# Turning a slot's rows with VectorE's 32x32 transposes in place of TensorE's, in a retention layer with a mixture of experts

## The chip, the cores and the metric

The kernel runs on one core of one Trainium2 chip. The metric is the device time of one execution in microseconds. Three runs of the kernel before took 399.4, 401.86 and 402.07 us, median 401.86.

## The reference, cut to what matters

Two layers follow each other. The first is retention over 4 batches, 8 heads, 768 positions and a head size of 64; the second sends each of the 3072 tokens (512 features) to one of 8 experts.

```
state = gamma * state + k[t] v[t]^T          # per batch and head
y[t]  = q[t] state / sqrt(64)
x     = y as 3072 rows of 512
logits = x @ w_gate + modality_bias[modality_id];  e = argmax(logits)
gate   = softmax(logits)[e]
out[rows of e] = gate * (relu(x[rows of e] @ w1[e]) @ w2[e])   # 512 -> 1024 -> 512
```

The order of the 512 features of `x` and of the rows of `w1` may be changed together without changing the product.

## The kernel before, in words

**Attention.** The 3072 tokens are 24 chunks of 128. For each chunk TensorE computes scores (`scores`, L168), products with the state (`heads_s`, L192) and with the masked scores (`heads_a`, L204), and VectorE masks the scores into `abuf` (L173) and writes the chunk's result `yT` (L211, features on partitions). `tokens_out` multiplies `yT` with an identity beside the gate's weights (L221), so that a chunk's rows and logits come out with tokens on partitions; ScalarE copies them into a tile `xs` in two halves (L225), VectorE reduces the logits (L226). ScalarE also scales the decay table into `dq` (L150), of which two buffers exist; chunk n's `dq` is read by `yT` of chunk n. From the third chunk on two chunks go together (`two_chunks`).

**Routing.** Per 6 chunks VectorE finds each token's expert and its place. GpSimd then writes the token's number and gate into the row and scatters the 128 rows of a chunk to `xsl` in HBM (L375). A row of `xsl` is 2176 bytes: four pieces of 128 features, each followed by 8 spare numbers; the first spare holds the token's number, the second its gate. `xsl` is divided into slots of 512 rows, each of one expert. The tile `xs` has ten buffers in rotation.

**Jobs.** A job is one slot through its expert. Two early jobs (`e0`, `e1`, full slots) and four from the final list (`f0` to `f3`) run in a row; a loop for further full slots exists. Two small remainders (`rest_...`, at most 32 rows) are computed inside the third and fourth job. A job has 32 stretches of six matmuls 128x128x512: 16 for `first` (L698, `w1`) and 16 for `second` (L716, `w2`). Each operand is split into a rounded part `hi` and a remainder `lo`, and three of their four products are taken. Beside them run, for the next job:
- `rows_in` (L646): SP loads the slot's 512 rows as four tiles `xg0` to `xg3` of 128 rows.
- `ids` (L656): VectorE copies the tokens' numbers and gates out of them, eight small copies.
- `raw` (L664) loads a weight block into one of four buffers; `cut` (L669) has ScalarE make `hi` (L672) and VectorE `lo` (L677).
- `flip` (L680), four calls: TensorE turns four 128x128 squares into one bank of PSUM (L683), ScalarE copies them to `hi` (L688), VectorE subtracts to get `lo` (L689).

At the end of a 128-row part of `second` ScalarE scales the result with the gate into `o` (L729), which uses the buffer of `xg0` to `xg3`, and GpSimd scatters it to the output (L730). `rest_flip` (L780) turns a remainder's 32 rows with four TensorE transposes (L781) and a ScalarE copy.

**Order.** On TensorE, ScalarE, VectorE and SP the order is that of the program text; GpSimd's instructions are pinned in order too. What belongs to a job is hung on named places: `at(n, where, ...)` puts a call at a place of chunk n, `on(q, ...)` at step q of a job (a step is two stretches, 16 steps to a job). The first job's `flip` calls stand at chunks 20 and 22, places "pr" (before `tokens_out` of the first chunk of the pair before) and "tk" (before that of the second); its `cut` calls at "end" of chunks 18 and 20, its `ids` at "end" of chunk 19. For every later job `rows_in` stands at step 5 of the job before it (step 1 for the second), `ids` at 8, `flip` at 8 and 9.

Of the kernel before, what the change touches and what calls it, by code (L numbers as in the profile page):

```python
# [7 lines left out]
F32 = mybir.dt.float32  # L8
F32R = mybir.dt.float32r
BF16 = mybir.dt.bfloat16  # L10
I32 = mybir.dt.int32
AF = mybir.ActivationFunctionType
ALU = mybir.AluOpType
AX = mybir.AxisListType

P = 128
B, H, S, D = 4, 8, 768, 64
NT, DM, NE, DF = B * S, H * D, 8, 1024
NCH = S // P
NN = B * NCH  # L20
NG = H // 2
GRP = 6
NGRP = NN // GRP
SLOT = 512
HH = SLOT // P
# [6 lines left out]
TAIL = 32  # L32
# [5 lines left out]
KC = DM // P  # L38
FC = DF // P
QW = KC * 256  # L40
LEAD = 12
XSB = 10
SINGLE = 2
XW = NG * (P + NE)
# [6 lines left out]
def kernel(  # L51
# [13 lines left out]
    nc = tc.nc  # L65
# [7 lines left out]
    wk = ctx.enter_context(tc.tile_pool(name="wk", bufs=2))  # L73
    me = ctx.enter_context(tc.tile_pool(name="me", bufs=1))
# [3 lines left out]
    def bank(name):  # L78
        return ps.tile([P, 512], F32, tag="bank", name=name)


    xsl = dr.tile([NONE + SLOT, XW], F32, name="xsl")
# [4 lines left out]
    ident = cst[:, C_ID : C_ID + P]  # L87
# [31 lines left out]
    def load_kq(n, split=False):  # L119
        tag = f"{('hi', 'lo')[n // 4 % 2]}{1 if n < 8 else 2}{n % 4}"  # L120
        t = me.tile([P, QW], F32R, tag=tag, name=f"kq_{n}")
        t = t.bitcast(F32).rearrange("p (i d) -> p i d", i=2)
# [512 lines left out]
    class Job:  # L635
        def __init__(self, tag):
            self.tag = tag
            self.raw, self.w, self.xT, self.hT = {}, {1: {}, 2: {}}, {}, []

    def reg(lst, i, hi):  # L640
        return nc.values_load(lst[0:1, i : i + 1], engines=[SP], min_val=0, max_val=hi)
# [2 lines left out]
        s.row, s.e = reg(lst, i, EMPTY) * SLOT, reg(lst, j, NE - 1)  # L644

    def rows_in(s):  # L646
        s.xg = [me.tile([P, XW], F32, tag=f"xg{hh}", name=f"xg{hh}_{s.tag}") for hh in range(HH)]
        src = xsl[bass.ds(s.row, SLOT), :].rearrange("(h p) w -> h p w", p=P)
        for hh in range(HH):
            ins = nc.sync.dma_start(s.xg[hh], src[hh])  # L650
            if s.tag[0] == "e":
                tc.add_to_no_dep_group("read_" + s.tag, ins.ins)
        if s.tag[0] == "e":
            reads.append("read_" + s.tag)

    def ids(s):  # L656
        s.tok = me.tile([P, HH], I32, tag="tok", name=f"tok_{s.tag}", bufs=2)
        s.gate = me.tile([P, HH], F32, tag="gate", name=f"gate_{s.tag}", bufs=2)
        for hh in range(HH):
            t = s.xg[hh]  # L660
            nc.vector.tensor_copy(s.tok[:, hh : hh + 1], t.bitcast(I32)[:, P : P + 1])
            nc.vector.tensor_copy(s.gate[:, hh : hh + 1], t[:, P + 1 : P + 2])

    def raw(s, m, i):  # L664
        src = w1 if m == 1 else w2
# [12 lines left out]
        s.w[m][i] = (hi, lo)  # L678

    def flip(s, kc):  # L680
        pb = bank(f"xp{kc}_{s.tag}")
        for hh in range(HH):
            nc.tensor.transpose(  # L683
                pb[:, hh * P : (hh + 1) * P], s.xg[hh][:, kc * (P + NE) : kc * (P + NE) + P], ident
            )
        t = me.tile([P, 2, SLOT], F32R, tag=f"xT{kc}", name=f"xT{kc}_{s.tag}")
        hi, lo = t[:, 0], t[:, 1]
        nc.scalar.copy(hi, pb)  # L688
        nc.vector.tensor_tensor(lo, pb, hi.bitcast(F32), op=ALU.subtract)  # L689
        s.xT[kc] = (hi, lo)  # L690

    def first(s, f, half):
        if half == 0:
# [17 lines left out]
    def second(s, hh, part):  # L711
        if part == 0:
            s.po = bank(f"o{hh}_{s.tag}")
        for f in range(2 * part, 2 * part + 2):
            for k, (a, wi) in enumerate(PAIRS):
                nc.tensor.matmul(  # L716
                    s.po, s.hT[f][a][:, hh * P : (hh + 1) * P],
                    s.w[2][f // 2][wi][:, (f % 2) * DM : (f % 2 + 1) * DM],
                    start=(f == 0 and k == 0), stop=(f == FC - 1 and k == 2),
                )  # L720
        if part == 3:
            o = me.tile([P, XW], F32, tag=f"xg{hh}", name=f"o{hh}_{s.tag}")[:, :DM]
            gate = s.gate[:, hh : hh + 1]
            if s is jobs[-1] and hh == HH - 1:
                h = DM // 2
                nc.vector.tensor_scalar(o[:, h:], s.po[:, h:], gate, None, op0=ALU.mult)
                nc.scalar.activation(o[:, :h], s.po[:, :h], AF.Copy, scale=gate)
            else:
                nc.scalar.activation(o, s.po, AF.Copy, scale=gate)  # L729
            ins = nc.gpsimd.indirect_dma_start(  # L730
                out=out[:, :],
                out_offset=bass.IndirectOffsetOnAxis(ap=s.tok[:, hh : hh + 1], axis=0),
                in_=o[:, :],
                in_offset=None,
                bounds_check=NT - 1,
                oob_is_err=False,
            )
            if s.tag != "dyn":
                disjoint(ins, "out_rows")
# [36 lines left out]
            nc.sync.dma_start(s.xg[g * TAIL : (g + 1) * TAIL], xsl[bass.ds(s.row, TAIL), :])  # L776

    def rest_flip(s):
        pb = bank("rxp")[:, : KC * TAIL].rearrange("p (c t) -> p c t", c=KC)
        for kc in range(KC):  # L780
            nc.tensor.transpose(  # L781
                pb[:, kc], s.xg[:TAIL, kc * (P + NE) : kc * (P + NE) + P], ident[:TAIL, :TAIL]
            )

        posf = me.tile([P, 1], F32, tag="rposf", name="rposf")
        nc.vector.tensor_copy(posf, s.xg.bitcast(I32)[:, P : P + 1])
        s.pos = me.tile([P, 1], I32, tag="rpos", name="rpos")
        nc.vector.scalar_tensor_tensor(s.pos, posf, 4.0, grp_t, op0=ALU.mult, op1=ALU.add)
        s.xT = wk.tile([P, KC, TAIL], F32, tag="s", name="rxT", bufs=3)
        nc.scalar.copy(s.xT, pb)  # L790

    def rest_first(s):
        ph = bank("rh")[:, :256]
# [50 lines left out]
    def at(n, where, fn, *args):  # L844
        hooks.setdefault((n, where), []).append((fn, args))
# [12 lines left out]
    for g in range(NGRP - 1):  # L858
        t = (g + 1) * GRP
# [8 lines left out]
        if early:  # L868
            at(t + 1, "end", early_b, g + 1)
            a, b = EARLY[g + 1]  # L870
# [5 lines left out]
    t = GRP * min(EARLY)  # L876
    at(t + 2, "st", taken_a)
    at(t + 2, "end", taken_b)
    e = jobs[0]
# [3 lines left out]
        at(t + 6 + 2 * i, "end", cut, e, 1, i)  # L883
        at(t + 7 + 2 * i, "top", raw, e, 2, i)
    at(t + 4, "sc", rows_in, e)
    at(t + 7, "end", ids, e)
    for kc in range(KC):
        at(t + 8 + kc // 2 * 2, ("pr", "tk")[kc % 2], flip, e, kc)

    def loads(n):  # L890

# [115 lines left out]
    def hooks_of(k):  # L1007

        hk = {}

        def on(q, fn, *args):
            hk.setdefault(q, []).append(lambda: fn(*args))

        s = jobs[k]
        for i in range(4):
            if k == 0 and i > 1:
                on(2 * i - 2, cut, s, 1, i)
                on(2 * i - 2, raw, s, 2, i)
            on(2 * i + 1, cut, s, 2, i)
        if k + 1 < len(jobs):  # L1020
            nxt = jobs[k + 1]
            on(1 if k == 0 else 5, rows_in, nxt)
            on(8, ids, nxt)
            for i in range(4):
                on(2 * i + 1, raw, nxt, 1, i)
                on(8 + i // 2, flip, nxt, i)
                on(9 + 2 * i, cut, nxt, 1, i)
                on(9 + 2 * i, raw, nxt, 2, i)
        if k == NEARLY - 2:

            on(3, gaps_room)
            on(6, gaps_a)
            on(7, gaps_b)
            on(7.5, gaps_c)
            for e in range(-1, NE):
                on(8 + (e + 1) / 2, gap, e)
        for s, load_in in zip(rests, (NEARLY - 1, NEARLY)):
            if k == load_in:
                on(7, rest_in, s)
                for i in range(8):  # L1040
                    on(7 + i, rest_load, s, 1 + i // 4, i % 4)
            if k == load_in + 1:
                on(0, rest_flip, s)
                on(2, rest_first, s)
                on(4, rest_mid, s)
                on(6, rest_second, s)
        if k == len(jobs) - 1:
            on(10, lambda: pin(nc.gpsimd.drain()))
        return hk
# [5 lines left out]
    with tc.manual_schedule(engines={PE, ACT, DVE, SP}):  # L1055
# [25 lines left out]
        r = last_tokens()  # L1081
# [7 lines left out]
    with tc.For_i(NLAST, nun, 1) as iv:  # L1089
        s = Job("dyn")  # L1090
        s.e = nc.values_load(
            lst[0:1, bass.ds(iv + U, 1)], engines=[SP], min_val=0, max_val=NE - 1
        )
        s.row = nc.values_load(
            lst[0:1, bass.ds(iv, 1)], engines=[SP], min_val=0, max_val=EMPTY
        ) * SLOT
        rows_in(s)
        ids(s)
        for kc in range(KC):
            flip(s, kc)  # L1100
        for m in (1, 2):
            for i in range(4):
                raw(s, m, i)
                cut(s, m, i)
        for i in range(32):
            stretch(s, i)


def _layout(inputs):
    import numpy as np  # L1110

    f = np.float32
# [10 lines left out]
    t = np.arange(S, dtype=np.float64) + 1.0  # L1123
# [7 lines left out]
    p = np.arange(P)  # L1131
    e = np.minimum(p // RUN, NE - 1)
# [8 lines left out]
    order = (head * D + np.arange(P) % D).reshape(DM)  # L1141
# [11 lines left out]
    mod = np.asarray(inputs["moe_modality_id"]).astype(np.int64).reshape(NN, P)  # L1153
    wg = inputs["moe_w_gate"][order].reshape(NG, P, NE).transpose(1, 0, 2)
    mb = np.broadcast_to(inputs["moe_modality_bias"].reshape(1, 2, NE), (P, 2, NE))
    w1 = inputs["moe_w1"][:, order].reshape(NE, KC, P, 4, 256).transpose(0, 3, 2, 1, 4)
    w2 = inputs["moe_w2"].reshape(NE, 4, 2, P, DM).transpose(0, 1, 3, 2, 4)
    arrs = {
        "qkv": np.stack([feat(k), feat(q), toks(k), toks(v)], axis=2),
# [45 lines left out]
```

## Time and profile before

| | |
|---|---|
| median of three runs | 401.86 us |
| profiled execution, its own time | 402.62 us |
| span of that execution | 400.8 us |
| mean granted TensorE clock | 0.994 of full |
| busy: TensorE / VectorE / ScalarE / GpSimd | 383.6 / 187.8 / 155.6 / 96.7 us |
| chain that ended last: TensorE / "issue" / DMA | 46% / 32% / 12% |

Busy time is summed over the span. A matmul's span overlaps the next one's, so TensorE's busy time says only when it had work. In a row of the timeline the columns are the start, the length, engine, line, operation, output from inputs, shape, count, and in brackets the idle time before it and what ended it. "issue" in the chain is time in which the engine waited for nothing that the profile shows.

### The profile page before, as it was taken

What the parts mean: (1) busy time and instruction counts of PE and PEld (TensorE: products, weight loads), DVE (VectorE), ACT (ScalarE), POOL (GpSimd) and SP (SyncE); (2) the same over time, 40 slices, a digit from 0 to 9 for tenths busy, and PEclk for the clock granted to TensorE, in tenths of its full rate; (3) what the DMA queues carried; (4) which work ended last, traced back from release to release, by engine and by line L of the source; (5) the groups of instructions that cost most, each with busy time, mean ns of one, the idle gap of its engine ahead of it and who ended that gap; (6) DMA issues with size and microseconds to landing.
All of it is one profiled execution on the core that took longest, in us unless ns stands there. A gap on an engine that the chain in (4) does not pass through costs nothing.

```text
span 400.8 us, 8169 instructions
## 1 busy us (share of the span) xinstructions
PE 383.6 (96%) x3067; PEld 323.2 (81%) x3067; DVE 187.8 (47%) x434; ACT 155.6 (39%) x305; POOL 96.7 (24%) x140
## 2 busy tenths in 40 slices
PE   4999999799999999999999999999999999999993
PEld 3999888698887888888877888878888888888882
DVE  1676858768649952445223352233622463234200
ACT  1255535336845432345223452334523443243110
POOL 1342581832810875000110001100011000100010
PEclk9999999899999999999999999999999999999999
DMA  7999899794545759367952579525343443400011
GB/s 273 398 385 398 303 339 400 239 390 174 198 147 189 248 184 330 116 216 243 370 201 81 198 243 359 214 71 199 105 159 105 156 166 131 151 35 0 15 39 50
DMA packets 27947, 82.32 MB, mean 205 GB/s; under 512 B 4861, under 2 KB 4989, under 8 KB 27649
## 3 DMA queue, kind: packets, MB, share of 16 engines
q1 hardware_dynamic: 22336, 66.09, 47.4%
q0 software_dynamic: 5136, 15.21, 9.8%
q8 instruction: 26, 0.43, 0.4%
q10 hardware_dynamic: 432, 0.46, 0.4%
q14 instruction: 17, 0.14, 0.1%
HBM read 65.42 MB, written 23.41 MB: 222 GB/s over the span
## 4 chain that ended last, share of the span: by engine, by line
PE 46%; issue 32%; DMA 12%; POOL 4%; DVE 3%; ACT 1%; POOLq 1%; SPq 0%; ACTq 0%
PE h_e L698 11%; PE o_e L716 11%; DMA kq<-in_qkv_dram 6%; DMA kv<-in_qkv_dram 6%; PE h_f L698 6%; PE o_f L716 5%; PE x L221 4%; POOL out_dram L730 3%; PE y L204 2%; PE sc L168 2%; PE y L192 1%; PE st L240 1%; PE xp_f L683 1%; PE xp_e L683 1%; DVE yT L211 1%
## 5 line engine op out<-in xcount | busy, mean ns | idle before, releaser
L698 PE MATMUL h_f<-xT_f,hi_f 128*128 128x512 f32 x256 | 81.3, 393 | 0.0
L716 PE MATMUL o_f<-hi_f,hT_f 128*128 128x512 f32 x256 | 79.4, 391 | 0.0
L677 DVE TENSOR_TENSOR lo_f<-raw_f,hi_f 128x1024 fp32r<-128x1024 f32 x32 | 39.2, 1224 | 49.5 <-ACT hi_f L672 45.3
L698 PEld LDWEIGHTS h_f<-xT_f,hi_f 128*128 128x128 f32 x256 | 48.1, 188 | 11.1 <-issue 1.2
L716 PEld LDWEIGHTS o_f<-hi_f,hT_f 128*128 128x128 f32 x256 | 47.6, 188 | 9.6
L706 DVE SCALAR_TENSOR_TENSOR hT_f<-h_f,hT_f 128x512 fp32r<-128x512 f32 x32 | 22.2, 692 | 66.4 <-ACT hT_f L705 66.4
L698 PE MATMUL h_f<-xT_f,lo_f 128*128 128x512 f32 x128 | 49.9, 390 | 0.0
L716 PE MATMUL o_f<-lo_f,hT_f 128*128 128x512 f32 x128 | 49.9, 390 | 0.0
L730 POOL DMA_INDIRECT out_dram<-o_f,tok_f x16 | 15.6, 972 | 132.6 <-ACT o_f L729 117.8
L698 PE MATMUL h_e<-xT_e,hi_e 128*128 128x512 f32 x128 | 40.5, 392 | 0.0
L705 ACT ACTIVATE hT_f<-h_f 128x512 fp32r<-128x512 f32 x32 | 19.2, 599 | 54.9 <-PE h_f L698 54.9
L716 PE MATMUL o_e<-hi_e,hT_e 128*128 128x512 f32 x128 | 39.8, 392 | 0.0
L173 DVE TENSOR_TENSOR abuf<-sc,cst 128x512 f32<-128x512 f32 x48 | 30.0, 681 | 17.4 <-PE sc L168 17.4
L156 POOL TENSOR_TENSOR vd<-kv,cst 128x512 f32<-128x512 f32 x24 | 24.9, 1045 | 42.5 <-PE y L204 13.5
L672 ACT CAST hi_f<-raw_f 128x1024 fp32r<-128x1024 f32 x32 | 33.4, 1045 | 0.0
L168 PE MATMUL sc<-kq 64*128 64x128 f32 x384 | 27.7, 293 | 5.4 <-DMA kq<-in_qkv_dram 5.2
L729 ACT ACTIVATE o_f<-o_f,gate_f 128x512 f32<-128x512 f32 x15 | 10.3, 689 | 55.0 <-PE o_f L716 43.6
L168 PEld LDWEIGHTS sc<-kq 64*128 64x128 f32 x384 | 24.6, 199 | 7.3 <-DMA kq<-in_qkv_dram 5.2
L221 PE MATMUL x<-wgt,yT 128*128 128x136 f32 x192 | 26.6, 287 | 3.1 <-DVE abuf L173 2.9
L225 ACT COPY xs<-x 128x272 f32<-128x272 f32 x48 | 18.4, 388 | 26.3 <-PE x L221 18.8
L716 PEld LDWEIGHTS o_f<-lo_f,hT_f 128*128 128x128 f32 x128 | 24.0, 188 | 5.0
L698 PEld LDWEIGHTS h_e<-xT_e,hi_e 128*128 128x128 f32 x128 | 24.0, 188 | 4.9
(172 smaller groups left out, 536.7 us busy)
## 6 DMA issues: line engine op xcount, KB each, us to landing
raw_f<-in_w_dram SPq DMA_DIRECT2D x32, 512.0 KB, 3.5
kq<-in_qkv_dram SPq DMA_DIRECT2D x23, 512.0 KB, 8.1
kv<-in_qkv_dram SPq DMA_DIRECT2D x19, 512.0 KB, 9.6
raw_e<-in_w_dram SPq DMA_DIRECT2D x16, 512.0 KB, 4.4
xg_f<-xsl SPq DMA_DIRECT2D x16, 272.0 KB, 4.4
abuf<-in_w_dram SPq DMA_DIRECT2D x8, 512.0 KB, 6.8
rw<-in_w_dram SPq DMA_DIRECT2D x16, 256.0 KB, 5.4
xg_e<-xsl SPq DMA_DIRECT2D x8, 272.0 KB, 4.2
```

Of the source, the lines that this page charges most:

```text
L156: nc.gpsimd.tensor_tensor(vds[n], vv, dec[:, n % NCH].unsqueeze(2).to_broadcast([P, H, D]), op=ALU.mult)
L168: nc.tensor.matmul(pe[j][:, g * P : (g + 1) * P], kt[r, g], qt[r, g], start=True, stop=True, skip_group_check=True,)
L173: nc.vector.tensor_tensor(a[:, j], pe[j].rearrange("p (h t) -> p h t", t=P), mask.unsqueeze(1).to_broadcast([P, NG, P]), op=ALU.mult,)
L221: nc.tensor.matmul(px[:, g], yT[:, 2 * u + g], wgt[:, 2 * u + g], start=(g == 0), stop=(g == 1), skip_group_check=True,)
L225: nc.scalar.copy(xs[:, 2 * u : 2 * u + 2], px)
L672: nc.scalar.copy(hi, t)
L677: nc.vector.tensor_tensor(lo, t, hi.bitcast(F32), op=ALU.subtract)
L698: nc.tensor.matmul(s.ph, s.w[1][f // 2][wi][:, o : o + P], s.xT[kc][a], start=(kc == 0 and k == 0), stop=(kc == KC - 1 and k == 2),)
L705: nc.scalar.activation(hi, s.ph, AF.Relu)
L706: nc.vector.scalar_tensor_tensor(lo, s.ph, 0.0, hi.bitcast(F32), op0=ALU.max, op1=ALU.subtract)
L716: nc.tensor.matmul(s.po, s.hT[f][a][:, hh * P : (hh + 1) * P], s.w[2][f // 2][wi][:, (f % 2) * DM : (f % 2 + 1) * DM], start=(f == 0 and k ...
L730: ins = nc.gpsimd.indirect_dma_start(out=out[:, :], out_offset=bass.IndirectOffsetOnAxis(ap=s.tok[:, hh : hh + 1], axis=0), in_=o[:, :], i ...
```

## The change

A job's rows are loaded as one tile `xb`, in which partition 32g + t holds, for each of 16 blocks of 32 rows, piece g (128 features) of row t of the block. VectorE turns the 32x32 squares of it, so that the features of one 128-row operand of the matmul are 32 from each of the four pieces; the rows of `w1` are laid out on the host in that order. The tokens' numbers and gates come by a load of their own (`tg`), and `ids` is gone. `flip` is divided: the transpose and ScalarE's copy stay at the old place, the subtraction `flip_lo` comes at a later one. The turned rows go through a buffer of the `xs` rotation. The output tile `o` is one for all four parts and shares its buffer with `xb`. `rest_flip` uses four VectorE transposes that write the operand directly.

```diff
+SQ = 32
+NB = SLOT // SQ
...
     def rows_in(s):
-        s.xg = [me.tile([P, XW], F32, tag=f"xg{hh}", name=f"xg{hh}_{s.tag}") for hh in range(HH)]
-        src = xsl[bass.ds(s.row, SLOT), :].rearrange("(h p) w -> h p w", p=P)
-        for hh in range(HH):
-            ins = nc.sync.dma_start(s.xg[hh], src[hh])
-            if s.tag[0] == "e":
+        s.xb = me.tile([P, NB, P], F32, tag="xb", name=f"xb_{s.tag}")
+        s.tg = me.tile([P, HH, 2], F32, tag="tg", name=f"tg_{s.tag}", bufs=2)
+        rows = xsl[bass.ds(s.row, SLOT), :]
+        src = rows.rearrange("(b t) (g e) -> g t b e", t=SQ, g=NG)
+        got = [
+            nc.sync.dma_start(s.xb[g * SQ : (g + 1) * SQ], src[g][:, :, :P]) for g in range(NG)
+        ]
+        got.append(
+            nc.sync.dma_start(s.tg, rows.rearrange("(h p) w -> p h w", p=P)[:, :, P : P + 2])
+        )
...
-    def ids(s):
-        s.tok = me.tile([P, HH], I32, tag="tok", name=f"tok_{s.tag}", bufs=2)
-        s.gate = me.tile([P, HH], F32, tag="gate", name=f"gate_{s.tag}", bufs=2)
-        for hh in range(HH):
-            t = s.xg[hh]
-            nc.vector.tensor_copy(s.tok[:, hh : hh + 1], t.bitcast(I32)[:, P : P + 1])
-            nc.vector.tensor_copy(s.gate[:, hh : hh + 1], t[:, P + 1 : P + 2])
...
     def flip(s, kc):
-        pb = bank(f"xp{kc}_{s.tag}")
-        for hh in range(HH):
-            nc.tensor.transpose(
-                pb[:, hh * P : (hh + 1) * P], s.xg[hh][:, kc * (P + NE) : kc * (P + NE) + P], ident
-            )
         t = me.tile([P, 2, SLOT], F32R, tag=f"xT{kc}", name=f"xT{kc}_{s.tag}")
-        hi, lo = t[:, 0], t[:, 1]
-        nc.scalar.copy(hi, pb)
-        nc.vector.tensor_tensor(lo, pb, hi.bitcast(F32), op=ALU.subtract)
-        s.xT[kc] = (hi, lo)
+        x = s.x[kc] = wk.tile([P, XW], F32, tag="xs", name=f"x{kc}_{s.tag}", bufs=XSB)[:, :SLOT]
+        nc.vector.transpose(
+            x.rearrange("p (b t) -> p b t", t=SQ), s.xb[:, :, kc * SQ : (kc + 1) * SQ]
+        )
+        nc.scalar.copy(t[:, 0], x)
+        s.xT[kc] = (t[:, 0], t[:, 1])
+
+    def flip_lo(s, kc):
+        hi, lo = s.xT[kc]
+        nc.vector.tensor_tensor(lo, s.x.pop(kc), hi.bitcast(F32), op=ALU.subtract)
...
-            o = me.tile([P, XW], F32, tag=f"xg{hh}", name=f"o{hh}_{s.tag}")[:, :DM]
-            gate = s.gate[:, hh : hh + 1]
+            if hh == 0:
+                s.o = me.tile([P, HH, DM], F32, tag="xb", name=f"o_{s.tag}")
+            o = s.o[:, hh]
+            gate = s.tg[:, hh, 1:2]
...
     def rest_flip(s):
-        pb = bank("rxp")[:, : KC * TAIL].rearrange("p (c t) -> p c t", c=KC)
-        for kc in range(KC):
-            nc.tensor.transpose(
-                pb[:, kc], s.xg[:TAIL, kc * (P + NE) : kc * (P + NE) + P], ident[:TAIL, :TAIL]
-            )
...
-        nc.scalar.copy(s.xT, pb)
+        for g in range(NG):
+            r, o = slice(g * TAIL, (g + 1) * TAIL), g * (P + NE)
+            nc.vector.transpose(
+                s.xT[r], s.xg[r, o : o + P].rearrange("p (c t) -> p c t", c=KC)
+            )
...
-    at(t + 7, "end", ids, e)
     for kc in range(KC):
         at(t + 8 + kc // 2 * 2, ("pr", "tk")[kc % 2], flip, e, kc)
+        at(t + 8 + kc // 2 * 2, ("tk", "end")[kc % 2], flip_lo, e, kc)
...
-            on(8, ids, nxt)
             for i in range(4):
                 on(2 * i + 1, raw, nxt, 1, i)
                 on(8 + i // 2, flip, nxt, i)
+                on(8.5 + i // 2, flip_lo, nxt, i)
...
-    w1 = inputs["moe_w1"][:, order].reshape(NE, KC, P, 4, 256).transpose(0, 3, 2, 1, 4)
+    w1 = inputs["moe_w1"][:, order].reshape(NE, NG, KC, SQ, 4, 256)
+    w1 = w1.transpose(0, 4, 1, 3, 2, 5)
```

## Rows read from the trace of the kernel before

**Rows 1.** The page, busy time of each engine (share of the span) and instructions.
```profile
PE 383.6 (96%) x3067; PEld 323.2 (81%) x3067; DVE 187.8 (47%) x434; ACT 155.6 (39%) x305; POOL 96.7 (24%) x140
```

**Rows 2.** Stretches: length, busy PE, PEld, DVE, ACT, POOL, clock, DMA share, GB/s.
```profile
96.00:112.00 16.00, 15.61 (x223) 13.85 (x222) 12.24 (x38) 10.54 (x30) 11.19 (x21) 1.00 0.48 172
112.00:394.00 282.00, 282.00 (x1452) 231.11 (x1450) 112.51 (x220) 101.80 (x150) 44.28 (x52) 1.00 0.48 166
```

**Rows 3.** The chain of waits in the jobs: start us, us, what.
```profile
181.03 0.87 PE xp_f L683 x8
...
204.63 0.36 PE rxp L781 x4
```

**Rows 4.** Timeline of VectorE, 98 to 106 us.
```profile
98.15 0.11 DVE L661 COPY tok_e<-xg_e 128x1 int32<-128x1 int32 x1
...
98.55 0.14 DVE L662 COPY gate_e<-xg_e 128x1 f32<-128x1 f32 x1
98.61 2.47 DVE L173 TENSOR_TENSOR abuf<-sc,cst 128x512 f32<-128x512 f32 x4
101.00 0.68 DVE L689 TENSOR_TENSOR xT_e<-xp_e,xT_e 128x512 fp32r<-128x512 f32 x1
...
102.31 0.20 DVE L226 TENSOR_REDUCE lg<-xs 128x8 f32<-128x32 f32 x1
103.83 1.23 DVE L677 TENSOR_TENSOR lo_e<-raw_e,hi_e 128x1024 fp32r<-128x1024 f32 x1 [1.33 <-ACT hi_e L672]
104.97 1.41 DVE L211 TENSOR_TENSOR yT<-y,dq 128x256 f32<-128x256 f32 x4
```

**Rows 5.** Timeline of ScalarE, 98 to 104 us.
```profile
98.64 0.59 ACT L688 CAST xT_e<-xp_e 128x512 fp32r<-128x512 f32 x1 [2.03 <-PE xp_e L683]
99.15 0.81 ACT L225 COPY xs<-x 128x272 f32<-128x272 f32 x2
...
101.59 1.27 ACT L150 ACTIVATE dq<-dcq,cst 128x128 f32<-128x128 f32 x4
102.77 1.03 ACT L672 CAST hi_e<-raw_e 128x1024 fp32r<-128x1024 f32 x1
```

**Rows 6.** Timeline of TensorE, 105 to 112 us.
```profile
105.53 1.17 PE L221 MATMUL x<-wgt,yT 128*128 128x136 f32 x8 [0.19 <-DVE yT L211]
...
110.93 1.19 PE L221 MATMUL x<-wgt,yT 128*128 128x136 f32 x8
111.87 0.48 PE L698 MATMUL h_e<-xT_e,hi_e 128*128 128x512 f32 x1
```

**Rows 7.** Timelines of GpSimd, SP, VectorE, TensorE in the jobs; the output's landing.
```profile
160.27 0.98 POOL L730 DMA_INDIRECT out_dram<-o_e,tok_e  x1 [2.67 <-ACT o_e L729]
...
170.94 0.33 SPq L650 DMA_DIRECT2D xg_f<-xsl  x1
...
185.77 1.29 DVE L689 TENSOR_TENSOR xT_f<-xp_f,xT_f 128x512 fp32r<-128x512 f32 x2 [0.51 <-ACT xT_f L688]
...
204.92 0.50 PE L698 MATMUL h_f<-xT_f,hi_f 128*128 128x512 f32 x1
...
out_dram<-o_e,tok_e POOLq DMA_INDIRECT x8, 5.5
```

**Rows 8.** TensorE's wait before 73.41, and the stretch around it as in rows 2.
```profile
73.41 0.73 PE L221 MATMUL x<-wgt,yT 128*128 128x136 f32 x4 [2.88 <-DVE abuf L173]
...
72.00:80.00 8.00, 6.59 (x98) 5.88 (x100) 5.28 (x18) 3.11 (x10) 6.70 (x14) 0.79 0.73 208
```

**Rows 9.** VectorE's groups by line and form: count, busy us, mean ns.
```profile
L256 DVE COPY wgt<-cst 128x512 f32<-128x512 f32 x1 | 0.4, 420 | 0.0
```

**Rows 10.** First job's row loads on SP, their landing, the stretch as in rows 2.
```profile
86.80 1.95 SPq L650 DMA_DIRECT2D xg_e<-xsl  x4
...
DMA to landing us min/median/max: 2.7/4.2/7.3
...
84.00:92.00 8.00, 8.00 (x148) 7.34 (x142) 4.62 (x12) 3.56 (x12) 2.09 (x2) 1.00 1.02 401
```

More of the change, by code (lines that the diff above doesn't have):

```diff
@@ L637, in __init__ @@
             self.tag = tag
-            self.raw, self.w, self.xT, self.hT = {}, {1: {}, 2: {}}, {}, []
+            self.raw, self.w, self.x, self.xT, self.hT = {}, {1: {}, 2: {}}, {}, {}, []
     def reg(lst, i, hi):
@@ L646, in rows_in @@
     def rows_in(s):
-        s.xg = [me.tile([P, XW], F32, tag=f"xg{hh}", name=f"xg{hh}_{s.tag}") for hh in range(HH)]
-        src = xsl[bass.ds(s.row, SLOT), :].rearrange("(h p) w -> h p w", p=P)
-        for hh in range(HH):
-            ins = nc.sync.dma_start(s.xg[hh], src[hh])
-            if s.tag[0] == "e":
+        s.xb = me.tile([P, NB, P], F32, tag="xb", name=f"xb_{s.tag}")
[8 more added lines that the diff above has]
+        )
+        if s.tag[0] == "e":
+            for ins in got:
                 tc.add_to_no_dep_group("read_" + s.tag, ins.ins)
-        if s.tag[0] == "e":
             reads.append("read_" + s.tag)
-    def ids(s):
-        s.tok = me.tile([P, HH], I32, tag="tok", name=f"tok_{s.tag}", bufs=2)
-        s.gate = me.tile([P, HH], F32, tag="gate", name=f"gate_{s.tag}", bufs=2)
-        for hh in range(HH):
-            t = s.xg[hh]
-            nc.vector.tensor_copy(s.tok[:, hh : hh + 1], t.bitcast(I32)[:, P : P + 1])
-            nc.vector.tensor_copy(s.gate[:, hh : hh + 1], t[:, P + 1 : P + 2])
     def raw(s, m, i):
@@ L731, in second @@
                 out=out[:, :],
-                out_offset=bass.IndirectOffsetOnAxis(ap=s.tok[:, hh : hh + 1], axis=0),
-                in_=o[:, :],
+                out_offset=bass.IndirectOffsetOnAxis(ap=s.tg.bitcast(I32)[:, hh, 0:1], axis=0),
+                in_=o,
                 in_offset=None,
@@ L1097 @@
         rows_in(s)
-        ids(s)
         for kc in range(KC):
             flip(s, kc)
+            flip_lo(s, kc)
         for m in (1, 2):
```

## The prediction

> **What bounds the kernel now.** I read the page's totals first: TensorE is busy for 96% of the span, VectorE for 47% [rows 1]. That is a mean over two stages, so the table by stretches comes next. From 112 us to 394 us, the expert jobs, TensorE is busy for all 282 us at full clock and VectorE for 112.5 us of them; in the 16 us before, where attention ends and the first job's rows are turned, TensorE is still busy for 15.6 us but VectorE for 12.2 and ScalarE for 10.5 [rows 2]. The chain of waits tells how close each stretch is. In the jobs it runs through TensorE alone, the transposes included [rows 3]. Around 100 us it is different: the three engine timelines show TensorE, ScalarE and VectorE handing work to each other within fractions of a microsecond, all three in written order [rows 4 to 6]. So an instruction taken off TensorE is worth its full time in the jobs, and perhaps nothing, or less, around 100 us.
>
> **What leaves TensorE in the jobs.** Eight transposes (two calls of `flip`) hold TensorE for 0.87 us in the chain, twice per job [rows 3]. Five jobs (the second early one and the four from the final list) are turned inside this stretch: 10 x 0.87 = 8.70 us. `rest_flip` holds it for 0.36 us [rows 3], twice: 0.72. Together **-9.42 us**.
>
> **What is added there, and its cover.** Per job VectorE gets four transposes and loses the eight small copies of `ids`; `flip_lo` is the old subtraction from another source, ScalarE's copy likewise. What they produce is finished at 187 and first used at 204.92 [rows 7], so some 18 us of other matmuls hide them. Without that cover each would cost its own duration. The same cover takes a late row load: SP issues the rows at 170.9 and they are wanted from 181.0 [rows 3, 7]; if they come late VectorE and ScalarE stand still, behind them wait `cut` and the output scaling, and behind `cut` SP's weight loads, but TensorE wants none of it before 204.92. The output tile now shares the row tile's buffer, so SP's row loads wait for the last output scatter of the job before: issued at 160.27, done 0.98 later, landed 5.5 after that, 166.8 [rows 7], still before 170.9. `rest_flip`'s four VectorE transposes replace a ScalarE copy two steps (5 us) ahead of their use. SP issues five loads for four and the pieces are shorter. The turned rows take buffers of the `xs` rotation, which GpSimd's scatters free: by order the third takes chunk 12's, scattered at chunk 20, one pair earlier. All this I cost at 0.
>
> **What happens around 100 us.** This is the step that I expect to give most of the gain back. Before, the first job's `flip` was TensorE, then ScalarE's copy, and the copy ran at 98.64 beside VectorE's mask products (98.61 to 101.0) [rows 4, 5]. Afterwards the copy needs VectorE's transpose, which stands behind those products in VectorE's order. I follow that order as the changed code writes it, with the durations of the old rows and one transpose at 0.68 us.
> First pair of chunks. Without `ids` (98.15 to 98.61) VectorE is free at 101.0 - 0.46 = 100.54. Then, each waiting for the one before: transpose 0.68, ScalarE copy 0.59, two `xs` copies 0.81, the logits' reduction 0.20, `flip_lo` 0.68, transpose 0.68, copy 0.59, two `xs` copies 0.81, four `dq` 1.27, `cut`'s copy 1.03, `cut`'s subtraction 1.23, the second `flip_lo` 0.68: 9.25 us [rows 4, 5]. Neighbours on one engine overlap a little (four products of 0.68 take 2.47 [rows 4]), so I take 9.0: `yT`, at 104.97 before, starts at about **109.6**.
> Second pair. Four `yT` 1.41, then transpose, copy, `xs` copies, reduction, `flip_lo` (0.68 + 0.59 + 0.81 + 0.20 + 0.68) twice, less the second reduction, which lies beside, then half of `yT` 0.42 before TensorE may start `x`: 7.55, with the overlaps 7.5: **117.1** where TensorE began it at 110.93 [rows 6]. That is a delay of **+6.2 us** for all that follows. TensorE's own work between, 105.53 to 110.93 less the transposes, is 4.5 us [rows 6] and fits underneath. The first job's 16 transposes (16 x 0.87 / 8 = 1.74 us) leave TensorE here too, and I count nothing for them: it would only wait longer.
> The clock. TensorE will stand still from about 103.4 to 110. [...]
>
> **The unknown prices.** No row shows a VectorE 32x32 transpose. From below: a plain copy of 128x512 takes 0.42 [rows 9]. From above: 16 blocks, each paid like the smallest VectorE instruction at 0.14 [rows 4], 2.24. I take the 0.68 of a 128x512 pass with one result per element, which it is nearest to in columns and type. Four stand in the chain, so the ends are -1.0 and +6.2 us.
> [...]
> The row load of the first job turns 512 rows of 2176 bytes into 2048 pieces of 512 bytes and 512 of 8. It was issued at 86.8 and landed at most 7.3 us after an issue, with the engines at 401 GB/s [rows 10]. If speed goes by bytes it lands near 95, hidden by 5 us, cost 0. If each piece takes as long as a whole row did, 1.1 MB at 401 GB/s is 2.8 us and three more such are 8.4: about 104, 3.5 us after VectorE wants it.
>
> **The sum.** The profiled execution took 402.62 us. 402.62 - 9.42 + 6.2 + 0.8 = 400.2. It stands 0.76 above the median of the runs, so against 401.86 I predict **399.4 us**, 0.6% faster.
>
> **The rivals.**
> 1. The whole gain. If VectorE and ScalarE find slack around 100 us that I don't see, the delay is nothing, and the first job's transposes leave TensorE's path too, 1.74 us. 402.62 - 9.42 - 1.74 = 391.5, or 390.7 against the median. For it: TensorE busy 96%. Against it: VectorE's order, in which the reduction that waits for ScalarE stands between the two transposes. Chance 0.15.
> 2. Slower: a costly transpose. [...] It decides from the point where four excesses over 0.68 eat the 2.4 us: 1.28 us per transpose. For it: no row of the kind. Against it: the plain 128x512 forms are all below 0.7. Chance 0.10.
> 3. Late rows. The small pieces land at 104 and VectorE stops the whole chain by 3.5 us: 403.7, or 402.9. For it: the engines were full when the load was issued. Against it: 13.7 us from issue to use. Chance 0.13.
> That the transposes would not leave TensorE can't be: the instructions are gone from the code.
>
> **Chances and range.** My forecast has 0.62; its own range is 396 to 402.5 (a transpose of 0.42 with no clock loss gives 397.6, hand-offs a little shorter 396; one near 1.2, 401.5). What can be told from no change is 1% of the median, 4 us: 397.8 to 405.9. Faster: rival 1 and a quarter of the forecast, 0.15 + 0.16, rounded to 0.32. Slower: most of rival 2 and what the others leave, 0.11. Within 1%: 0.57. The range 394 to 404.5 takes in the forecast, rival 3 and the cheaper half of rival 2; rival 1 lies outside.
>
> **What would show it.** Right: TensorE without transposes and gapless from the first `h` matmul to the end, over about 272.6 us instead of 282; the first `h` matmul near 118 to 119 instead of 111.87; `yT` of the 21st chunk near 109.6 with VectorE waiting for ScalarE's `xs` copies between two transposes; a granted clock under 1 between 104 and 120. Wrong: a first `h` matmul at 112 or before (rival 1); transposes over 1.3 us (rival 2); VectorE waiting for the row tile's DMA at 100 us (rival 3); or TensorE waiting inside the jobs, which would mean that the cover of 18 us isn't there.

## The result and the profile after

The changed kernel took **397.43 us** (median of 6 runs, 397.03 to 397.94), the kernel before on the same chip 401.16 us (6 runs, 399.4 to 402.07): ratio 0.9897, 95% interval 0.9882 to 0.9912. The prediction was 399.4 us and no change beyond 1%; the change gained 1.0%. The profiled execution took 397.86 us, 4.76 less than that of before.

The page of the changed kernel, the totals that answer to [rows 1]: busy time, share of the span, instructions.
```profile
PE 373.9 (94%) x2963; PEld 314.7 (79%) x2963; DVE 202.8 (51%) x418; ACT 156.5 (40%) x303; POOL 97.8 (25%) x140
```
TensorE has 104 instructions fewer: 96 transposes of the six jobs and 8 of the two remainders.

The table by stretches of the changed kernel, columns as in [rows 2]; the last row is the stretch of the jobs.
```profile
96.00:112.00 16.00, 10.53 (x126) 9.44 (x126) 10.19 (x25) 7.17 (x19) 9.53 (x19) 0.87 0.51 173
...
104.00:108.00 4.00, 0.51 (x10) 0.27 (x6) 1.66 (x3) 2.78 (x8) 3.31 (x8) 0.97 0.46 173
108.00:112.00 4.00, 3.15 (x14) 3.18 (x15) 2.74 (x8) 2.41 (x7) 1.09 (x1) 0.50 0.69 237
112.00:116.00 4.00, 4.00 (x60) 3.42 (x61) 2.43 (x6) 2.36 (x7) 0.84 (x1) 0.67 0.48 104
...
118.00:390.00 272.00, 271.63 (x1361) 222.05 (x1360) 125.64 (x209) 102.43 (x147) 45.10 (x52) 1.00 0.55 168
```
In the jobs TensorE is as full as before: the trace has no wait of it from 118 to 390 us. From 96 to 112 us its busy time fell from 15.61 to 10.53 us, though it lost only 16 transposes there (1.74 us): it stands still from 104.51 to 108.85 (the wait of 4.34 us below), and then runs at a granted clock of 0.50 from 108 to 112 and 0.67 from 112 to 116.

VectorE's timeline of the changed kernel, answering to [rows 4], and in its last row to VectorE's of [rows 7] (start, length, engine, line, operation, shape, count, idle time before it and what ended it).
```profile
97.43 2.44 DVE L175 TENSOR_TENSOR abuf<-sc,cst 128x512 f32<-128x512 f32 x4
99.79 0.70 DVE L685 STREAM_TRANSPOSE x_e<-xb_e 128x512 f32<-128x512 f32 x1
101.75 0.21 DVE L228 TENSOR_REDUCE lg<-xs 128x8 f32<-128x32 f32 x1 [1.26 <-ACT xs L227]
...
102.48 0.71 DVE L685 STREAM_TRANSPOSE x_e<-xb_e 128x512 f32<-128x512 f32 x1
104.44 0.20 DVE L228 TENSOR_REDUCE lg<-xs 128x8 f32<-128x32 f32 x1 [1.26 <-ACT xs L227]
106.54 1.23 DVE L678 TENSOR_TENSOR lo_e<-raw_e,hi_e 128x1024 fp32r<-128x1024 f32 x1 [1.90 <-ACT hi_e L673]
107.69 0.68 DVE L693 TENSOR_TENSOR xT_e<-x_e,xT_e 128x512 fp32r<-128x512 f32 x1
108.29 1.41 DVE L213 TENSOR_TENSOR yT<-y,dq 128x256 f32<-128x256 f32 x4
...
115.37 1.80 DVE L213 TENSOR_TENSOR yT<-y,dq 128x256 f32<-128x256 f32 x4 [0.30 <-PE y L206]
...
191.83 1.29 DVE L693 TENSOR_TENSOR xT_f<-x_f,xT_f 128x512 fp32r<-128x512 f32 x2
```
ScalarE's timeline of the changed kernel, answering to [rows 5].
```profile
100.53 0.62 ACT L688 CAST xT_e<-x_e 128x512 fp32r<-128x512 f32 x1 [4.64 <-DVE x_e L685]
101.05 0.67 ACT L227 COPY xs<-x 128x272 f32<-128x272 f32 x2
```
The two engines take turns as the prediction wrote it out. VectorE transposes at 99.79; ScalarE, which did the same copy at 98.64 before, now waits 4.64 us for that; VectorE then waits 1.26 us for ScalarE's `xs` copies before it comes to its next transpose. The first `yT` of the second pair of chunks starts at 108.29 instead of 104.97.

TensorE's timeline of the changed kernel, answering with its first row to [rows 8], then to [rows 6], and with the last two to TensorE's row of [rows 7] and to the end.
```profile
72.69 0.73 PE L223 MATMUL x<-wgt,yT 128*128 128x136 f32 x4 [2.88 <-DVE abuf L175]
...
97.23 2.12 PE L223 MATMUL x<-wgt,yT 128*128 128x136 f32 x16
...
108.85 3.96 PE L223 MATMUL x<-wgt,yT 128*128 128x136 f32 x16 [4.34 <-DVE yT L213]
...
116.56 1.19 PE L223 MATMUL x<-wgt,yT 128*128 128x136 f32 x8
117.50 0.48 PE L701 MATMUL h_e<-xT_e,hi_e 128*128 128x512 f32 x1
...
206.51 0.39 PE L701 MATMUL h_f<-xT_f,hi_f 128*128 128x512 f32 x1
...
389.24 0.39 PE L719 MATMUL o_f<-lo_f,hT_f 128*128 128x512 f32 x1
```
One group of 16 matmuls that took 2.12 us at 97.23 takes 3.96 at 108.85, behind the wait of 4.34 us. The first `h` matmul is at 117.50 instead of 111.87.

**Where the 4.76 us came from.** Split both executions at VectorE's becoming free of the mask products (100.54 before, without `ids`; 99.79 after), at the first `h` matmul, and at the start of the last `o` matmul (393.80 before, 389.24 after). Up to the first split: -0.75 us. From there to the first `h`: 11.33 before, 17.71 after, **+6.38**. Jobs: 281.93 before, 271.74 after, **-10.19**. Behind them: 8.82 before, 8.62 after, -0.20. Sum -4.76. The first term isn't the change's: TensorE's wait of 2.88 us ended at 73.41 before [rows 8] and ends at 72.69 after, 0.72 earlier, and the first instruction of the change, the row load, is issued at 85.71. The trace has the difference as early as 13 us: two groups of matmuls (`y` and `st` of the first chunks) took 1.97 and 1.01 us before, 1.68 and 0.63 after, and the `sc` matmuls behind them start at 13.76 and 13.04. E1 and E2 below, which hold most of the change, start those at 13.63 and 13.79, so this differs from execution to execution. In the experiments below VectorE comes free between 99.1 and 101.2 us.

### The profile page after: what moved, and what is told of

Its sections match the earlier page's. It is cut to its first block, busy times and chain, and to the rows that moved or that the text cites. A ratio compares the mean times of both kernels' runs of the same rounds, so it can differ in the third digit from the quotient of the medians.

```text
span 396.1 us, 7938 instructions
## 1 busy us (share of the span) xinstructions
PE 373.9 (94%) x2963; PEld 314.7 (79%) x2963; DVE 202.8 (51%) x418; ACT 156.5 (40%) x303; POOL 97.8 (25%) x140
## 4 chain that ended last, share of the span: by engine, by line
issue 56%; PE 24%; POOL 8%; DVE 6%; DMA 3%; ACT 1%; POOLq 1%; ACTq 0%; DVEq 0%
PE x L223 6%; POOL out_dram L735 5%; PE sc L170 5%; PE y L206 4%; PE h_e L701 4%; PE y L194 2%; PE st L242 2%; DMA kv<-in_qkv_dram 2%; DMA cst<-in_consts_dram 1%; POOL xsl L623 1%; POOL vd L158 1%; DVE x_e L685 1%; DVE abuf L175 1%; DVE lo_e L678 1%; ACT xs L227 1%
## 5 line engine op out<-in xcount | busy, mean ns | idle before, releaser
L735 POOL DMA_INDIRECT out_dram<-o_f,tg_f x16 | 15.5, 972 | 127.2 <-ACT o_f L734 116.9
L223 PE MATMUL x<-wgt,yT 128*128 128x136 f32 x192 | 28.0, 300 | 7.2 <-DVE yT L213 4.3
L223 PEld LDWEIGHTS x<-wgt,yT 128*128 128x128 f32 x192 | 25.1, 202 | 9.2 <-issue 4.7
```

The costliest lines, as they stand in the source:

```text
L223: nc.tensor.matmul(px[:, g], yT[:, 2 * u + g], wgt[:, 2 * u + g], start=(g == 0), stop=(g == 1), skip_group_check=True,)
L735: ins = nc.gpsimd.indirect_dma_start(out=out[:, :], out_offset=bass.IndirectOffsetOnAxis(ap=s.tg.bitcast(I32)[:, hh, 0:1], axis=0), in_=o, ...
```

## The experiments

Two sets of four kernels each ran beside the kernel before: 401.86 us in the first set (E1 to E4, 7 runs), 402.43 in the second (E5 to E8, 11 runs). Compare ratios, therefore, where sets differ. "Hand-offs" is the time from the first transpose of the first job (for the kernel before, VectorE's becoming free) to the first `h` matmul, "jobs" from there to the start of the last `o` matmul, both from the profiled execution.

| kernel | median us | ratio, 95% interval | hand-offs | jobs |
|---|---|---|---|---|
| before | - | 1 | 11.33 | 281.93 |
| changed | 397.43 | 0.9897 (0.9882 to 0.9912) | 17.71 | 271.74 |
| E1 first job on TensorE | 390.73 | 0.9719 (0.9703 to 0.9735) | - | 271.71 |
| E2 other order | 390.34 | 0.9705 (0.9687 to 0.9722) | 9.44 | 271.77 |
| E3 only the first job on VectorE | 406.99 | 1.0101 (1.006 to 1.0142) | 17.87 | 280.57 |
| E4 TensorE kept busy | 397.2 | 0.9888 (0.9871 to 0.9904) | 16.67 | 271.76 |
| E5 later transposes twice | 398.51 | 0.9897 (0.9878 to 0.9915) | 17.40 | 271.73 |
| E6 first transposes twice | 400.27 | 0.9944 (0.9928 to 0.996) | 19.66 | 271.76 |
| E7 remainders on TensorE | 399.82 | 0.9929 (0.9912 to 0.9946) | 17.65 | 272.99 |
| E8 other buffer | 398.44 | 0.9903 (0.9885 to 0.992) | 17.56 | 271.77 |

**E1 and E3: which job gains, which loses.** E1 turns the first job's rows on TensorE again, E3 those of all other full jobs instead (`on_pe` there is `s is not jobs[0] and s.tag != "dyn"`). A job turned by TensorE is loaded with tokens on partitions, still in pieces of 512 bytes, and its `w1` comes from a second copy in the old order of rows.
```diff
+    def on_pe(s):
+        return s is jobs[0]
...
     def flip(s, kc):
+        if on_pe(s):
+            pb = bank(f"xp{kc}_{s.tag}")
+            for hh in range(HH):
+                nc.tensor.transpose(pb[:, hh * P : (hh + 1) * P], s.xg[:, hh, kc], ident)
+            nc.scalar.copy(t[:, 0], pb)
+            nc.vector.tensor_tensor(t[:, 1], pb, t[:, 0].bitcast(F32), op=ALU.subtract)
...
-        src = w1 if m == 1 else w2
+        src = w2 if m == 2 else w1p if on_pe(s) else w1
```


> The changed kernel, but the first job alone is turned by TensorE again: its rows come with tokens on partitions in 512-byte pieces, its w1 from a second copy in the old order. Theory (the loss is the first job's turning on VectorE, in its written order around 100 us): the first h matmul comes near 111, the 10.2 us that the jobs gained stay, about 391 us. Rival A (the loss comes from the other parts of the change, the shorter pieces, the extra load of tokens and gates, the shared output buffer): the first h matmul stays near 117.5 and the time near 397.

> The reverse of the first: the first job is turned by VectorE as in the changed kernel, all later ones by TensorE as before (w1 from a copy in the old order for them); the remainders stay on VectorE. Theory: the loss of 5.6 to 6.3 us at the first h matmul is kept (117 to 118) and the gain of the jobs is gone but for the remainders' 1.1 us: 401.2 + 6.3 - 1.1, about 406. Rival A: near 402, since VectorE's turning of the first job costs nothing by itself.

TensorE's timeline of E1:
```profile
105.03 1.17 PE L224 MATMUL x<-wgt,yT 128*128 128x136 f32 x8 [0.28 <-DVE yT L214]
...
111.37 0.48 PE L723 MATMUL h_e<-xT_e,hi_e 128*128 128x512 f32 x1
```
TensorE's timeline of E3:
```profile
109.81 3.96 PE L224 MATMUL x<-wgt,yT 128*128 128x136 f32 x16 [4.34 <-DVE yT L214]
...
118.62 0.48 PE L723 MATMUL h_e<-xT_e,hi_e 128*128 128x512 f32 x1
...
399.19 0.39 PE L741 MATMUL o_f<-lo_f,hT_f 128*128 128x512 f32 x1
```
With the first job alone back on TensorE the wait of 4.34 us is gone (0.28 is left) and the whole saving of the jobs stays: 390.73 us. With the first job alone turned by VectorE the wait is there, unchanged, and only the two remainders' saving is left against it: slower than before (four runs from 403.89 to 407.51 us, the interval of the ratio above 1). Rival A falls in both. So the delay is the first job's, and the gain that of the others. E3's jobs also price the transposes on TensorE: 280.57 - 271.74 = 8.83 us for ten groups of eight, 0.88 us a group.

**E2: the order, not the amount.** The first job keeps VectorE's transposes, but they stand where VectorE would otherwise wait: two at the end of the 21st chunk, before `cut`, two beside the next `yT`; the copies and subtractions follow later, so that ScalarE's `xs` copies no longer stand behind a copy that waits for a VectorE transpose. The turned rows lie in the idle buffers `hT4` to `hT7`. In the edit `turn` is the transpose alone and `flip_hi` ScalarE's copy alone.
```diff
+    for kc in range(2):
+        at(t + 8, "end", turn, e, kc)
     for i in range(2):
         at(t + 6 + 2 * i, "end", cut, e, 1, i)
...
-    for kc in range(KC):
-        at(t + 8 + kc // 2 * 2, ("pr", "tk")[kc % 2], flip, e, kc)
-        at(t + 8 + kc // 2 * 2, ("tk", "end")[kc % 2], flip_lo, e, kc)
+    for kc in range(2):
+        at(t + 8, "end", flip_hi, e, kc)
+        at(t + 10, "st", turn, e, kc + 2)
+        at(t + 10, "end", flip_hi, e, kc + 2)
+    for kc in range(2):
+        at(t + 10, "st", flip_lo, e, kc)
+        at(t + 11, "end", flip_lo, e, kc + 2)
```


> The changed kernel with the same instructions for the first job in another order: two transposes after both logits reductions of chunk 20's pair, ScalarE's copies behind cut's copy, the other two transposes and two subtractions after yT of chunk 21, the last two subtractions after yT of chunk 23; the turned rows lie in buffers that are idle then. Theory (order): VectorE has 4 to 5 us idle between 100 and 109 and takes the work there, TensorE never waits long, first h matmul near 110 and 390 us in all. Rival B (amount: 2.8 us more of VectorE's time cannot be placed in a stretch where it is busy for three quarters): first h matmul at 114 or later, 394 us or more.

VectorE's timeline of E2:
```profile
100.82 1.30 DVE L694 STREAM_TRANSPOSE x_e<-xb_e 128x512 f32<-128x512 f32 x2
102.66 1.23 DVE L678 TENSOR_TENSOR lo_e<-raw_e,hi_e 128x1024 fp32r<-128x1024 f32 x1 [0.53 <-ACT hi_e L673]
103.80 1.41 DVE L213 TENSOR_TENSOR yT<-y,dq 128x256 f32<-128x256 f32 x4
```
TensorE's timeline of E2:
```profile
104.36 2.09 PE L223 MATMUL x<-wgt,yT 128*128 128x136 f32 x16 [0.67 <-DVE yT L213]
...
110.26 0.48 PE L713 MATMUL h_e<-xT_e,hi_e 128*128 128x512 f32 x1
```
The same transposes, subtractions and copies now leave VectorE one wait of 0.53 us instead of waits of 1.26, 1.26 and 1.90 up to the first `yT` (103.80 instead of 108.29), and TensorE waits 0.67 instead of 4.34. Rival B falls, and the kernel is 2.95% under the one before. Counted from VectorE's becoming free, as for the kernel before, the hand-offs are 9.73 us here (from 100.53; two reductions come ahead of the transposes) and 11.01 in E1 (from 100.36). So in the profiled executions the first job gains 1.28 us over E1, where TensorE still has its 16 transposes. The medians, 390.34 and 390.73, don't tell the two apart.

**E8: the buffer alone.** E2 changed both the order and where the turned rows lie, so E8 changes only the latter.
```diff
-        x = s.x[kc] = wk.tile([P, XW], F32, tag="xs", name=f"x{kc}_{s.tag}", bufs=XSB)[:, :SLOT]
+        if s is jobs[0]:
+            u = me.tile([P, 2, SLOT], F32R, tag=f"hT{4 + kc}", name=f"x{kc}_{s.tag}")
+            x = u.bitcast(F32)[:, 0]
+        else:
+            x = wk.tile([P, XW], F32, tag="xs", name=f"x{kc}_{s.tag}", bufs=XSB)[:, :SLOT]
+        s.x[kc] = x
```


> The changed kernel in its own order, with only the first job's turned rows placed in idle hT buffers, as the reordered kernel (390.34 us) had them, in place of the xs rotation. Theory (the order of the instructions made the reordered kernel's gain, the place of the turned rows nothing): no change, 397.4 us, first h matmul near 117.5. Rival F (waiting for buffers of the xs rotation is what delays the first job): most of the 7.1 us comes back, first h matmul near 111 and the time near 391 us.

TensorE's timeline of E8:
```profile
109.71 3.97 PE L223 MATMUL x<-wgt,yT 128*128 128x136 f32 x16 [4.34 <-DVE yT L213]
```
Ratio 0.9903 for the changed kernel's 0.9897, hand-offs 17.56 us for 17.71, TensorE's wait again 4.34: the buffers of the `xs` rotation cost nothing, and rival F falls. E2's gain is the order's.

**E4: what the clock costs.** Seventeen matmuls, whose result nothing reads, keep TensorE busy while it waits for the first pair.
```diff
+    def warm(s):
+        pb = bank("warm")
+        for _ in range(17):
+            nc.tensor.matmul(pb, s.w[1][0][0][:, :P], s.xT[0][0], start=True, stop=True)
+
+    at(t + 10, "st", warm, e)
```


> The changed kernel with 17 matmuls that nobody reads put on TensorE (3.85 us at full clock) in its wait of 4.3 us before yT of chunk 20. Theory (of the 5.6 us about 0.9 is the half clock between 108 and 115 that the wait brings): granted clock 1.0 there, first h matmul near 116.6, 396.5 us. Rival C (VectorE's chain sets the end there whatever the clock): 117.5 and 397.4, unchanged.

TensorE's timeline of E4:
```profile
105.65 4.46 PE L893 MATMUL warm<-xT_e,hi_e 128*128 128x512 f32 x17
109.94 2.01 PE L223 MATMUL x<-wgt,yT 128*128 128x136 f32 x16
...
115.49 1.17 PE L223 MATMUL x<-wgt,yT 128*128 128x136 f32 x8 [0.60 <-DVE yT L213]
```
The table by stretches of E4, columns as in [rows 2]:
```profile
108.00:112.00 4.00, 4.00 (x30) 3.52 (x32) 2.74 (x8) 2.41 (x7) 1.09 (x1) 1.00 0.62 201
```
VectorE's timeline of E4:
```profile
99.73 0.71 DVE L685 STREAM_TRANSPOSE x_e<-xb_e 128x512 f32<-128x512 f32 x1 [0.61 <-DMA xb_e<-xsl]
```
The granted clock from 108 to 112 us is 1.00 for 0.50. The group of 16 takes 2.01 us for 3.96, TensorE is ahead and waits 0.60 for `yT`, where in the changed kernel VectorE waited 0.30 for TensorE. The hand-offs are 1.04 us shorter, where 0.9 was expected. The medians don't show it (397.2 and 397.43 for an expected 396.5; the ratios' intervals overlap), so the clock's price stands on these rows alone. The last row gives a part of the reason: VectorE came free at 99.12, 0.67 us earlier than in the changed kernel's trace, and waited 0.61 for the first job's rows, for which it didn't wait there. Counted from 99.12 only 0.43 of the 1.04 us is left. Whether the other executions lost it in the same way is not shown.

**E5: is VectorE's new work in the jobs covered?** Every transpose of the other full jobs is done twice.
```diff
-        nc.vector.transpose(
+        for _ in range(1 if s is jobs[0] else 2):
+            nc.vector.transpose(
```


> The changed kernel (397.43 us), with every VectorE transpose of the four full jobs after the first early one done twice, 20 or fewer more instructions of 0.69 us. Theory (some 18 us of other matmuls cover VectorE's work in the jobs): the same time, 397.4 us within 0.5, and 271.7 us from the first h matmul to the start of the last o matmul as before the edit. Rival C (the cover is smaller than that, and part of the transposes is paid for in the jobs): up to 20 x 0.69 = 13.8 us more, and TensorE waits for VectorE's xT ahead of an h matmul.

VectorE's groups by line in E5 (count, busy us, mean ns, idle time before):
```profile
L686 DVE STREAM_TRANSPOSE x_f<-xb_f 128x512 f32<-128x512 f32 x32 | 21.8, 699 | 0.6
```
VectorE's and TensorE's timelines of E5, the last `lo` of the third job's rows and their first use:
```profile
196.43 0.69 DVE L694 TENSOR_TENSOR xT_f<-x_f,xT_f 128x512 fp32r<-128x512 f32 x1 [0.17 <-ACT xT_f L689]
...
207.53 0.39 PE L702 MATMUL h_f<-xT_f,hi_f 128*128 128x512 f32 x1
```
Twenty more transposes, some 13.8 us of VectorE's time, leave the jobs at 271.73 us and the ratio at 0.9897. The rows are done at 197.12 and wanted at 207.53: 10.4 us of cover are left. This experiment's rival C falls.

**E6: the price of a transpose in the chain.** The same doubling for the first job alone (`2 if s is jobs[0] else 1`).

> The changed kernel, with the four VectorE transposes of the first job alone done twice. Theory (all four stand in the chain in which VectorE and ScalarE hand work to each other, each at its own 0.6 to 0.69 us): 4 x 0.6 to 4 x 0.69 = 2.4 to 2.8 us later, the first h matmul near 120.1 and the time near 400.0 us. Rival D (VectorE waits in that chain for ScalarE and has room to spare): no change, first h matmul near 117.5, 397.4 us.

VectorE's timeline of E6:
```profile
100.39 1.45 DVE L686 STREAM_TRANSPOSE x_e<-xb_e 128x512 f32<-128x512 f32 x2
...
110.37 1.41 DVE L213 TENSOR_TENSOR yT<-y,dq 128x256 f32<-128x256 f32 x4
```
TensorE's timeline of E6:
```profile
110.94 3.96 PE L223 MATMUL x<-wgt,yT 128*128 128x136 f32 x16 [3.49 <-DVE yT L213]
...
119.13 1.17 PE L223 MATMUL x<-wgt,yT 128*128 128x136 f32 x8 [0.30 <-DVE yT L213]
```
The first pair is 1.48 us longer (9.98 for 8.50 from the transpose to `yT`), two transposes at 0.74. The second pair adds only 0.48 (8.19 for 7.71 between the two `x` rows): there TensorE at its lower clock (a granted 0.50 from 108 to 112 us in the changed kernel) had been the last, and the rest of VectorE's extra work fits beside it. In all 1.95 us, and the ratio rises by 0.0047, 1.9 us. Rival D falls; the theory's 2.4 to 2.8 was too high, because it took all four for the chain's.

**E7: what a remainder's transposes cost TensorE.** Two remainders on TensorE again, with the second copy of `w1` for them.
```diff
-        for g in range(NG):
-            r, o = slice(g * TAIL, (g + 1) * TAIL), g * (P + NE)
-            nc.vector.transpose(s.xT[r], s.xg[r, o : o + P].rearrange("p (c t) -> p c t", c=KC))
+        pb = bank("rxp")[:, : KC * TAIL].rearrange("p (c t) -> p c t", c=KC)
+        for kc in range(KC):
+            nc.tensor.transpose(
+                pb[:, kc], s.xg[:TAIL, kc * (P + NE) : kc * (P + NE) + P], ident[:TAIL, :TAIL])
+        nc.scalar.copy(s.xT, pb)
```


> The changed kernel, with the two remainders' rows turned by TensorE again as before the change, with a second copy of w1 in the old order for them. Theory (a transpose in the middle of the jobs costs TensorE its own time and a gap in restarting, 0.56 us each by the matmul starts of the trace before): 2 x 0.56 = 1.1 us more, 398.5 us; from the first h matmul to the start of the last o matmul 272.9 us for 271.7. Rival E (only the 0.36 us that the chain of waits showed for each): 0.7 us more, 398.1 us and 272.5 us.

TensorE's timeline of E7, around the first remainder's transposes:
```profile
207.13 0.61 PE L720 MATMUL o_e<-hi_e,hT_e 128*128 128x512 f32 x2
207.59 0.39 PE L720 MATMUL o_e<-lo_e,hT_e 128*128 128x512 f32 x1
207.91 0.43 PE L793 MATMUL rxp<-cst,rx 32*128 32x32 f32 x4
208.26 0.50 PE L702 MATMUL h_f<-xT_f,hi_f 128*128 128x512 f32 x1
208.61 0.40 PE L702 MATMUL h_f<-xT_f,lo_f 128*128 128x512 f32 x1
```
The jobs are 1.25 us longer, 0.62 per remainder; rival E's 0.36 is too little. The rows say why. In an even run a matmul starts every 0.23 us (two from 207.13 to 207.59): behind the one of 207.59 the next two would have started at 207.82 and 208.05. They start at 208.26 and 208.61, 0.56 late at the second: 0.09 are lost ahead of the transposes and 0.12 behind the first matmul after them. The remaining 0.06 per remainder is not accounted for. The ratio, 0.9929 for 0.9897, agrees (1.3 us) but couldn't decide by itself.

## Why the prediction was right or wrong

The mechanism was right in its main steps, several sizes were off, nearly all in the same direction: for the profiled execution the sum gave 400.2 us, and it took 397.86, 2.34 less. That carried the result from a forecast gain of 0.6% to one of 1.0% (0.88 to 1.18% by the interval), onto the edge of the 1% within which the prediction spoke of no change. The step that failed is the sum's first term, TensorE's relief in the jobs: it was taken as -9.42 us, because `rest_flip` was priced by its own piece of the chain, and measured -10.19. The hand-offs, 0.62 too long, are the next.

1. **What leaves TensorE in the jobs: mis-sized, -9.42 forecast, -10.19 measured.** The price of the eight transposes, 0.87 us [rows 3], holds: E3 gives 0.88. That of `rest_flip`, 0.36 [rows 3], doesn't: E7 gives 0.62. The chain's piece is the time that the transposes held TensorE; the matmuls around them lose a little more at both ends, 0.09 and 0.12 us in E7's rows, and this stood in no piece named after the transposes. By the experiments 8.83 + 1.25 = 10.08. Of the 0.77 us that the forecast lacked the remainders make 0.53 (1.25 for 0.72) and the groups of eight 0.13 (8.83 for 8.70); the last 0.11 is not accounted for.
2. **The cover in the jobs: right.** Nothing on TensorE waits for the turned rows; they are finished at 193.12 (191.83 + 1.29) and first used at 206.51, 13.4 us of the 18 forecast. E5 shows that even twice the work fits.
3. **The hand-offs around 100 us: right in kind, 0.6 too long.** Forecast +6.2 and the clock's +0.8, 7.0; measured +6.38, of which E4's hand-offs leave 5.34 (16.67 - 11.33) to the order and 1.04 to the clock. The first pair took 8.50 us (99.79 to 108.29) for 9.0: ScalarE's two `xs` copies take 0.67 us for the 0.81 of [rows 5], where TensorE was done with the second half only at 99.53, and neighbours on ScalarE overlap by 0.10 each (the copy of 0.62 from 100.53 and the `xs` copies from 101.05). The second pair can be read in E4, where TensorE isn't late: 7.26 us from `yT` (108.23) to `x` (115.49), for 7.5. E1 shows that the delay is the first job's, E2 and E8 that it comes from the order alone.
4. **The clock: right, +0.8 forecast, 1.0 by the rows of E4.** No run shows the sum's +0.8, which was the author's estimate; E4's hand-offs show 1.04 us in its place, or 0.43 counted from VectorE's becoming free. The wait behind which the granted clock fell to 0.50 (108 to 112 us) was 4.34 us, and the same group of matmuls took 3.96 for 2.12.
5. **The unknown price: right, 0.68 taken, 0.69 measured.** VectorE's groups by line in the changed kernel (count, busy us, mean ns, idle time before):
```profile
L685 DVE STREAM_TRANSPOSE x_f<-xb_f 128x512 f32<-128x512 f32 x16 | 10.4, 686 | 0.0
L792 DVE STREAM_TRANSPOSE rxT<-rx 32x128 f32<-32x128 f32 x8 | 2.4, 302 | 0.1
```
The pass over 512 elements per partition took as long as the subtraction of that shape (0.69; 0.68 in [rows 4]), not the 2.24 of sixteen blocks; only the plain copy was shorter, 0.42 [rows 9]. (The upper end called 0.14 the smallest VectorE instruction; one of [rows 4] took 0.11, which would have made it 1.76.) Rival 2 falls.

6. **The row load: hidden, with nothing to spare.** SP's timeline of the changed kernel, answering to SP's rows of [rows 10] and [rows 7]:
```profile
85.71 3.81 SPq L655 DMA_DIRECT2D xb_e<-xsl  x4
89.72 2.85 SPq L658 DMA_DIRECT2D tg_e<-xsl  x1
...
174.84 1.94 SPq L655 DMA_DIRECT2D xb_f<-xsl  x4
176.98 0.94 SPq L658 DMA_DIRECT2D tg_f<-xsl  x1
```
Landing of the early jobs' rows in the changed kernel, answering to [rows 10]:
```profile
DMA to landing us min/median/max: 3.6/6.9/10.0
```
The first job's issues ran to 89.5 us, and a load landed up to 10.0 us after its issue. VectorE's transpose at 99.79 didn't wait for it; in E4 it did, for 0.61 us. The forecast of 5 us to spare was too good, rival 3's 3.5 us late too bad.

7. **The base.** Up to the first split the profiled execution after was 0.75 us quicker than that of before, which no instruction of the change explains; it is there at 13 us already. Medians are moved likewise: 401.86 of the three runs known, 401.16 of six, 401.86 and 402.43 in the later sets. Against 401.16 the same sum would have given 398.7 us.

Together: 0.77 us from the jobs, 0.62 from the hand-offs with the clock, 0.75 from the start and 0.20 from the end make the 2.34. Between the medians, where each side has several executions, the gain is 3.73 us (401.16 to 397.43) for the 2.46 forecast; the jobs' 0.77 and the hand-offs' 0.62 make 1.39, about the 1.27 that are missing there, without the base. Rival 1, no delay at all, had the result on its side of the forecast but not its reason: this kernel has the delay. Its number, 390.7 us, is what the kernel takes when the delay is taken out (E2, 390.34 us). The argument against it, that the reduction which waits for ScalarE stands between two transposes, named the very thing that E2 moves.

## What to carry to other kernels

Price an instruction that leaves a full engine by when its neighbours start without it, not by its own piece of the chain: for eight transposes the two agreed (0.88 and 0.87 us), for a remainder's short group they didn't (0.62 and 0.36). When work moves to an engine with a low mean load, follow that engine's written order through the stretch where it hands work back and forth: here VectorE, busy for 47% of the span, cost 6.4 us with the clock's part, and the same instructions in another order cost nothing (E2). Where a change gains in one place and loses in another, split it by place first: E1 and E3 found with two kernels what each part was worth.

## What the runs showed of the hardware

- A VectorE transpose of 32x32 blocks, float32, 128x512, took 0.69 us; two in a row into different tiles 1.30 (E2), into the same tile 1.45 (E6). 32x128 took 0.30.
- In every kernel that had TensorE's wait of 4.34 us the granted clock of 108 to 112 us was 0.50 to 0.65 (0.50 in the changed kernel, 0.65 in E3, 0.56 in E5, 0.63 in E7, 0.54 in E8), and the group of 16 matmuls behind that wait took 3.96 us (3.97 in E8) for 2.12. In E4, after a wait of 1.82 us that ended at 101.43, the granted clock of 104 to 108 was 0.71 although TensorE had work for all 4 us of it; in E6, after one of 1.87 that ended at 102.83, it was 0.65.
- The load of 512 eight-byte pieces (`tg`, 4 KB) held SP for 0.94 us in the jobs and 2.85 us at 89.72, where a quarter of the rows (256 KB in pieces of 512 bytes) took 0.49 us (1.94 / 4) and 0.95 (3.81 / 4). The early jobs' rows landed after 6.9 us in the median, before the change after 4.2 [rows 10].
